# Filling, key order and value spacing in a one-core attention and gated feed-forward kernel

## The chip, the cores and the metric

The kernel runs on one core of one Trainium2 chip. The metric is the device time of one execution in microseconds (us): before the change 269.87, 267.0 and 269.37 us in three runs, median 269.37 us. A further execution was recorded by the hardware profiler.

Five engines of the core run their own instruction lists and wait for each other by semaphores: PE (TensorE, matmuls; its weight loads stand apart as PEld), DVE (VectorE), ACT (ScalarE), POOL (GpSimd) and SP (SyncE, which here only issues DMAs; its rows carry SPq). POOL issues DMAs too.

## The reference

A batch of 4 sequences of 768 tokens has 8 heads of 64 numbers. Each query sees 8 global keys and the 96 keys up to itself; the scores get a penalty by distance and head. The attention's output, as 3072 rows of 512 numbers, goes through a gated feed-forward part.

```python
keep = is_global | is_local                      # pos < 8, or 0 <= rel < 96
scores = scale * q @ k.T - slopes * dist         # -1e9 where not keep
a = softmax(scores)
x = (a @ v).transpose(0, 2, 1, 3).reshape(B * S, H * D)      # 3072 x 512
gate = np.maximum(x @ w_gate, 0.0)               # 512 x 1536
val = x @ w_val
out = (gate * val) @ w_out                       # 1536 x 512
```

## The kernel before, in words

**The pieces.** The work is cut into eight chunks of 384 tokens, the halves of the four sequences (`s` or `c` = 0 to 7; sequence `b = s // 2`). The heads go in four pairs `p`. A sequence's keys are cut into seven tiles of 128 columns: the 8 global keys and 120 others. `kT[b % 2][p]` holds the transposed keys of a pair, `qTb[s % 2]` the transposed queries, with zeros in the other head's half, so that one matmul gives both heads.

**The values.** `vbuf[b % 2]` holds for each of the seven tiles a row of 17 blocks of 64 numbers: ones, values of head 0, ones, values of head 1, and so on to a last block of ones. A matmul with 128 columns of it gives a head's value product in one half of the partitions and the softmax's denominator in the other (`piece_av`, L327). Chunks 0 and 1 use `piece_av_wide` instead (L359), which takes ones from a tile of its own. `fill` (L136) writes ones over a whole tile, and the loads of values (`load_v_globals` L120, `load_v` L131, by POOL) write over the value blocks. `spread_v_globals` (L125, by SP) copies the rows of the global keys from the first tile into the others.

**One chunk of attention.** `piece_qk` makes scores (PE L299), their exponential (ACT L302) and the product with a mask of penalties (DVE L311). It is called three times for a pair, for three groups of key tiles. `piece_av` is called for each head of a pair (`e` = 0, 1): 4 or 5 matmuls, the logarithm of the denominator (ACT L336); with the second head one exponential for both (ACT L341) and two multiplications into `xT` (DVE L344). `av_psum` has two buffers, so the pair's two results are held until L344 has read them.

**Getting queries and keys.** Chunks 0 and 1 are transposed by PE: `piece_cast` (L222, on DVE in chunk 0, on POOL in chunk 1), six small matmuls (`piece_t`, L253), copies out of PSUM on DVE (L258, L259, and `put_keys` L237 to L243; L239 copies the 8 global keys into all seven tiles). From chunk 2 on `early_pieces(s)` does it: POOL casts queries (L266) and keys (L267), SP issues six transposing DMAs (queries L272, keys L275), and POOL puts the keys in order (`piece_order`, L237 to L243). The loads of queries and keys are issued by SP (L110).

**One chunk of feed-forward.** 24 pieces of four matmuls with 384 columns (gate L397, ACT L400; value L407, DVE L409), then six pieces of six matmuls with 512 columns (L416), in pairs; after each pair ACT copies the result (L421) and SP stores it.

**The order.** There is no scheduler: each engine runs its instructions in the order of the program text. `weave` merges lists: `spread` gives the attention pieces of the next chunk evenly spaced places in the current chunk's feed-forward work (0.0 to 0.88 of it, from L503 on), `early_pieces` of the chunk after that stand between 0.25 and 0.75. A list of n pieces is spaced by its length, so two more entries in it move all others. At the beginning (L457 to L470) `aside` says which fills, zeros and loads go ahead of which piece of chunk 0. PE then runs part of chunk 0's feed-forward work with chunk 1's attention in between (L485), a stretch of feed-forward work alone while POOL, SP and the DMAs get chunk 2 ready (L496, L497), and the rest with chunk 2's attention (L500).

Of the kernel before, what the change touches and what calls it, by code (L numbers as in the profile page):

```python
# [15 lines left out]
def kernel(  # L16
# [87 lines left out]
    def load_qk(s, h0, h1):  # L104
# [18 lines left out]
    def spread_v_globals(b, j0=1, j1=NT):  # L123
        t = vbuf[b % 2]
        nc.sync.dma_start(  # L125
            out=t[0:NG, j0:j1, :],
            in_=t[0:NG, 0:1, :].to_broadcast([NG, j1 - j0, (2 * H + 1) * D]))
# [7 lines left out]
    def fill(eng, i, j):  # L135
        eng.memset(vbuf[i][:, j, :].bitcast(mybir.dt.uint32), 0x3F803F80)  # L136
# [33 lines left out]
    fill(nc.vector, 0, 0)  # L170
# [33 lines left out]
    for p in range(2):  # L204
        nc.scalar.copy(qTb[0][64:128, p, 0, :], zeros[64:128])
        nc.scalar.copy(qTb[0][0:64, p, 1, :], zeros[0:64])
# [10 lines left out]
    def piece_cast(s, p):  # L217
        qk = cast_pool.tile([128, 2, NN, 2, D], BF16, name="qk")
        cast_of[s, p] = qk
        for i, src in ((0, qs_of[s]), (1, ks_of[s])):  # L220
# [41 lines left out]
    def piece_cast_all(s, p):  # L262

        qsrc = qs_of[s][:, 2 * p : 2 * p + 2, :].rearrange("t e (n d) -> t e n d", n=NN)
        for e in range(2):
            nc.gpsimd.tensor_copy(qz[s % 2][:, :, p, e, 64 * e : 64 * e + 64], qsrc[:, e])  # L266
        nc.gpsimd.tensor_copy(  # L267
            kc[s % 2].rearrange("t n (h d) -> t h n d", d=D)[:, 2 * p : 2 * p + 2],
            ks_of[s][:, 2 * p : 2 * p + 2, :].rearrange("t e (n d) -> t e n d", n=NN))

    def piece_x(s, n):
# [3 lines left out]
        nc.sync.dma_start_transpose(  # L275
            out=kNb[s % 2][:, :, n * 128 : (n + 1) * 128], in_=kc[s % 2][:, n])
# [95 lines left out]
    def attention_pieces(s):  # L372
# [11 lines left out]
        return QK(0) + QK(1) + AV(0) + QK(2) + AV(1) + QK(3) + AV(2) + AV(3)  # L384
# [68 lines left out]
    def zero_q(i, p):  # L453
        nc.gpsimd.memset(qTb[i][64:128, p, 0, :].bitcast(mybir.dt.uint32), 0)
        nc.gpsimd.memset(qTb[i][0:64, p, 1, :].bitcast(mybir.dt.uint32), 0)

    a0 = attention_pieces(0)  # L457
    aside = {
        1: [lambda: fill(nc.vector, 0, 1), lambda: fill(nc.vector, 0, 2),
            lambda: load_v_globals(0), lambda: load_v(0, 0), lambda: load_v(0, 1)],  # L460
        2: [lambda: nc.vector.memset(kT[0][0][:, 3, 32:128], 0.0), lambda: fill(nc.vector, 0, 3),
# [10 lines left out]
    for j in range(4, NT):  # L472
# [75 lines left out]
```

## Time and profile before

| | us |
|---|---|
| median of three runs (267.0 to 269.87) | 269.37 |
| the profiled execution, its whole time | 267.93 |
| its span, first to last instruction | 266.2 |
| PE busy in the span | 237.6 |
| DVE / ACT / POOL busy | 140.8 / 156.8 / 97.2 |

The profile's views: busy times by engine and by stretch, waits (which instruction stood idle before it, and what released it), and the timeline, whose rows give start, duration, engine, line, what is written and read, how many instructions were merged, and in square brackets the idle time ahead of them. A duration can hold time in which an instruction was held up, so unusual ones are to be looked at beside their neighbours. Line numbers with L are those of the kernel before, unless a text says otherwise; in the changed kernel the same statements stand up to 11 lines further on.

### The profile page before, as it was taken

What the parts mean: (1) busy time and instruction counts of PE and PEld (TensorE: products, weight loads), DVE (VectorE), ACT (ScalarE), POOL (GpSimd) and SP (SyncE); (2) the same over time, 40 slices, a digit from 0 to 9 for tenths busy, and PEclk for the clock granted to TensorE, in tenths of its full rate; (3) what the DMA queues carried; (4) which work ended last, traced back from release to release, by engine and by line L of the source; (5) the groups of instructions that cost most, each with busy time, mean ns of one, the idle gap of its engine ahead of it and who ended that gap; (6) DMA issues with size and microseconds to landing.
All of it is one profiled execution on the core that took longest, in us unless ns stands there. A gap on an engine that the chain in (4) does not pass through costs nothing.

```text
span 266.2 us, 4655 instructions
## 1 busy us (share of the span) xinstructions
PE 237.6 (89%) x1608; PEld 139.1 (52%) x1608; DVE 140.8 (53%) x366; ACT 156.8 (59%) x317; POOL 97.2 (37%) x237
## 2 busy tenths in 40 slices
PE   1268988999699899989999999989998999989994
PEld 0136645666355456645664566545664566546641
DVE  8985895444444366724574376616673366534410
ACT  8338585333367567746775567666774677653321
POOL 8892499050690653244241901516150400000000
PEclk9999999999999999999999999999999999999999
DMA  6999699995896599549629693267928200021012
GB/s 187 163 201 230 149 173 199 248 108 130 239 132 166 169 220 149 115 106 153 209 63 157 72 214 123 59 176 112 233 59 135 106 0 2 0 79 42 0 39 79
DMA packets 81198, 34.56 MB, mean 130 GB/s; under 512 B 56920, under 2 KB 77912, under 8 KB 81176
## 3 DMA queue, kind: packets, MB, share of 16 engines
q1 hardware_dynamic: 49320, 26.38, 36.8%
q0 software_dynamic: 31856, 7.91, 31.2%
q8 instruction: 12, 0.20, 0.3%
q14 instruction: 10, 0.08, 0.1%
HBM read 28.38 MB, written 6.29 MB: 130 GB/s over the span
## 4 chain that ended last, share of the span: by engine, by line
PE 71%; DVE 9%; DMA 6%; ACT 6%; SPq 2%; POOL 2%; issue 2%; DVEq 0%; ACTq 0%; POOLq 0%
PE ff_ps L416 20%; PE ff_ps L407 19%; PE ff_ps L397 19%; PE qk_ps L299 6%; PE av_ps L327 5%; DMA ks<-in_k_dram 5%; ACT lnd L336 2%; DVE xT L344 1%; DVE es L311 1%; DVE kT L239 1%; PE av_ps L359 1%; PE qk_ps L253 1%; SPq L272 1%; ACT rcp L341 1%; SPq L275 1%
## 5 line engine op out<-in xcount | busy, mean ns | idle before, releaser
L397 PE MATMUL ff_ps<-xT,wg 128*128 128x384 bf16 x384 | 78.5, 326 | 1.1 <-DVE xT L344 0.4
L407 PE MATMUL ff_ps<-xT,wv 128*128 128x384 bf16 x384 | 78.0, 326 | 0.0
L409 DVE TENSOR_TENSOR ht<-ff_ps,grelu 128x384 bf16<-128x384 f32 x96 | 53.3, 556 | 34.4 <-PE ff_ps L407 27.3
L400 ACT ACTIVATE grelu<-ff_ps 128x384 bf16<-128x384 f32 x96 | 47.0, 489 | 40.1 <-DVE ht L409 21.8
L416 PE MATMUL ff_ps<-wo_sb,ht 128*128 128x512 bf16 x288 | 68.1, 378 | 0.0
L302 ACT ACTIVATE es<-qk_ps 128x432 bf16<-128x432 f32 (+2 forms) x96 | 49.4, 529 | 28.3 <-PE qk_ps L299 25.9
L311 DVE TENSOR_TENSOR es<-es,m_all 128x432 bf16<-128x432 bf16 (+6 forms) x144 | 43.3, 392 | 29.5 <-ACT es L302 28.7
L344 DVE TENSOR_TENSOR xT<-av_ps,rcp 64x384 bf16<-64x384 f32 x48 | 26.7, 555 | 43.7 <-ACT rcp L341 43.0
L407 PEld LDWEIGHTS <-wv 128*128 128x128 bf16 x384 | 36.4, 98 | 23.4 <-issue 1.1
L397 PEld LDWEIGHTS <-wg 128*128 128x128 bf16 x384 | 36.6, 98 | 22.9 <-issue 0.3
L416 PEld LDWEIGHTS <-ht 128*128 128x128 bf16 x288 | 26.9, 97 | 27.7
L299 PE MATMUL qk_ps<-qT,kT 128*128 128x432 bf16 (+6 forms) x144 | 33.6, 303 | 4.2 <-POOL kT L239 2.6
L336 ACT ACTIVATE lnd<-av_ps 64x384 f32<-64x384 f32 x48 | 23.3, 486 | 9.7 <-PE av_ps L327 8.9
L421 ACT COPY osb<-ff_ps 128x512 f32<-128x512 f32 x24 | 14.1, 586 | 25.1 <-PE ff_ps L416 23.3
L266 POOL CAST qz<-qs 128x192 bf16<-128x192 f32 x48 | 16.3, 367 | 33.6 <-DMA qs<-in_q_dram 26.9
L327 PE MATMUL av_ps<-es,vbuf 128*128 128x216 bf16 (+4 forms) x216 | 20.6, 225 | 5.4 <-DVE xT L344 5.4
L131 POOL DMA_DIRECT2D vbuf<-in_v_dram x28 | 24.4, 879 | 0.8 <-DVE qk L222 0.6
L327 PEld LDWEIGHTS <-vbuf 128*128 128x128 bf16 x216 | 17.6, 97 | 13.6 <-issue 6.9
L299 PEld LDWEIGHTS <-kT 128*128 128x128 bf16 x144 | 14.3, 102 | 16.1 <-issue 3.8
L267 POOL CAST kc<-ks 128x384 bf16<-128x384 f32 x24 | 12.7, 531 | 13.3 <-DMA ks<-in_k_dram 13.3
L253 PE MATMUL qk_ps<-ident,qk 128*128 128x128 bf16 x48 | 5.5, 264 | 12.0 <-DVE qk L222 12.0
L237 POOL COPY kT<-kN 128x360 bf16<-128x360 bf16 x12 | 6.4, 537 | 26.1 <-DMA kN<-kc 26.1
(66 smaller groups left out, 124.9 us busy)
## 6 DMA issues: line engine op xcount, KB each, us to landing
out_dram<-osb SPq DMA_DIRECT2D x24, 256.0 KB, 2.2
qs<-in_q_dram SPq DMA_DIRECT2D x6, 768.0 KB, 6.3
ks<-in_k_dram SPq DMA_DIRECT2D x6, 768.0 KB, 8.6
vbuf<-in_v_dram POOLq DMA_DIRECT2D x24, 120.0 KB, 5.1
qs<-in_q_dram SPq DMA_DIRECT2D x8, 192.0 KB, 9.6
ks<-in_k_dram SPq DMA_DIRECT2D x8, 192.0 KB, 4.2
wg<-in_moe_w_gate_dram POOLq DMA_DIRECT2D x3, 512.0 KB, 5.7
wv<-in_moe_w_val_dram POOLq DMA_DIRECT2D x3, 512.0 KB, 7.5
```

The source lines that it names most:

```text
L131: nc.gpsimd.dma_start(out=v_dst(b, NG + r0, NG + r0 + n, j), in_=v[b, :, KT * j + r0 : KT * j + r0 + n, :].rearrange("h p d -> p h d"))
L299: nc.tensor.matmul(ps[:, c : c + n_], lhsT=kt[:, j, :], rhs=qd[:, :, :, a : a + w], start=True, stop=True)
L302: nc.scalar.activation(es[:, 0:cols], ps[:, 0:cols], AF.Exp, bias=0.0, scale=scale)
L311: nc.vector.tensor_mul(e4, e4, mk)
L327: nc.tensor.matmul(av3[:, :, a : a + w], lhsT=vb[:, j, z0 : z0 + 128], rhs=es[:, c : c + NN * w].rearrange("k (n p) -> k n p", n=NN), star ...
L336: nc.scalar.activation(ln[o0 : o0 + 64], av[d0 : d0 + 64, 0:QH], AF.Ln, bias=0.0, scale=1.0)
L344: nc.vector.tensor_tensor(xT_of[s][r, p, :], av_of[s, p, e_][r, 0:QH], rc[r], op=ALU.mult)
L397: nc.tensor.matmul(psg[:, 0:QH], lhsT=w_of(wg, dc, fc), rhs=xT[:, dc, :], start=(dc == 0), stop=(dc == N_DC - 1))
L400: nc.scalar.activation(gr, psg[:, 0:QH], AF.Relu, bias=0.0, scale=1.0)
L407: nc.tensor.matmul(psv[:, 0:QH], lhsT=w_of(wv, dc, fc), rhs=xT[:, dc, :], start=(dc == 0), stop=(dc == N_DC - 1))
L409: nc.vector.tensor_tensor(ht[:, fc, :], psv[:, 0:QH], st["gr"], op=ALU.mult)
L416: nc.tensor.matmul(ps2, lhsT=ht[:, fc, n * 128 : (n + 1) * 128], rhs=wo_sb[:, fc, :], start=(fc == 0), stop=(fc == N_FC - 1))
```

## The change

1. `fill` is gone. The value tiles of sequence 0 get no ones (chunks 0 and 1 don't read them); POOL clears the last tile, which no load fills wholly. Four fills on DVE and three on POOL at the beginning go away. The tiles of sequence 1 get their ones by `fill_ones`, which writes the nine blocks of ones alone (on POOL, after one clearing of the last tile); those of `vbuf[0]` get them later, on DVE, for sequence 2.
2. `spread_v_globals` copies only the value blocks, by one DMA for each tile: three and three in sequence 0, six in each of the others, in place of one DMA.
3. Keys are loaded ahead of queries in each pair of loads, and cast ahead of them. `early_pieces` does all keys' casts, then the three key transposes, then the queries' casts and transposes, then the ordering of keys: 18 pieces in place of 11.
4. The zeros in `qTb[0]` for pairs 2 and 3 are written by ACT, not POOL.
5. In chunks 2 to 7 the last pieces come in another order: the two value pieces of pair 2 stand between the three score pieces of pair 3, and two empty pieces ahead of the value pieces of pair 3.

```diff
-        for src, dst in ((q, qs_of[s]), (k, ks_of[s])):
+        for src, dst in ((k, ks_of[s]), (q, qs_of[s])):
...
     def spread_v_globals(b, j0=1, j1=NT):
-        t = vbuf[b % 2]
-        nc.sync.dma_start(
-            out=t[0:NG, j0:j1, :],
-            in_=t[0:NG, 0:1, :].to_broadcast([NG, j1 - j0, (2 * H + 1) * D]))
+        for j in range(j0, j1):
+            nc.sync.dma_start(out=v_dst(b, 0, NG, j), in_=v_dst(b, 0, NG, 0))
...
-    def fill(eng, i, j):
-        eng.memset(vbuf[i][:, j, :].bitcast(mybir.dt.uint32), 0x3F803F80)
+    def fill_ones(eng, i, j):
+        eng.memset(vbuf[i][:, j, :].bitcast(mybir.dt.uint32).rearrange(
+            "p (h z) -> p h z", z=D // 2)[:, 0 : 2 * H + 1 : 2, :], 0x3F803F80)
...
-    fill(nc.vector, 0, 0)
...
     def early_pieces(s):
-        out = [(0.0, lambda p=p: piece_cast_all(s, p)) for p in range(HP)]
-        out += [(0.0, lambda n=n: piece_x(s, n)) for n in range(NN)]
+        out = [(0.0, lambda p=p: piece_cast_k(s, p)) for p in range(HP)]
+        out += [(0.0, lambda n=n: piece_xk(s, n)) for n in range(NN)]
+        out += [(0.0, lambda p=p: piece_cast_q(s, p)) for p in range(HP)]
+        out += [(0.0, lambda n=n: piece_xq(s, n)) for n in range(NN)]
         out += [(0.0, lambda p=p: piece_order(s, p)) for p in range(HP)]
...
-        return QK(0) + QK(1) + AV(0) + QK(2) + AV(1) + QK(3) + AV(2) + AV(3)
+        g = QK(3)
+        a = AV(2)
+        return (QK(0) + QK(1) + AV(0) + QK(2) + AV(1) + g[0:1] + a[0:1] + g[1:2] + a[1:2] + g[2:3]
+                + [(0.0, lambda: None)] * 2 + AV(3))
...
-    for j in range(4, NT):
-        fill(nc.gpsimd, 0, j)
+    nc.gpsimd.memset(vbuf[0][:, NT - 1, :].bitcast(mybir.dt.uint32), 0)
...
+    nc.gpsimd.memset(vbuf[1][:, NT - 1, :].bitcast(mybir.dt.uint32), 0)
     for j in range(NT):
-        fill(nc.gpsimd, 1, j)
+        fill_ones(nc.gpsimd, 1, j)
...
-    weave(f1_0[G[1]] + f1_1[G[1]], spread(early_pieces(2), 0.0, 1.0))
+    weave(f1_0[G[1]] + f1_1[G[1]], spread(early_pieces(2), 0.0, 1.0),
+          [(0.1 + 0.12 * j, lambda j=j: fill_ones(nc.vector, 0, j)) for j in range(NT)])
```

**How the order moves, first place: ACT at the end of a chunk's attention** (here chunk 3's, woven into chunk 2's feed-forward work; `es` are the exponentials of scores, `lnd` and `rcp` the logarithm and the reciprocal of `piece_av`, each `osb` the end of two feed-forward pieces L416). Before:

```order
L302 ACTIVATE es_1614<-qk_ps 128x480
L400 ACTIVATE grelu<-ff_ps 128x384
L302 ACTIVATE es_1631<-qk_ps 128x480
L302 ACTIVATE es_1654<-qk_ps 128x432
L421 COPY osb<-ff_ps 128x512
L336 ACTIVATE lnd<-av_ps 64x384 x2
L341 ACTIVATE rcp<-lnd 128x384
L336 ACTIVATE lnd<-av_ps 64x384
L421 COPY osb<-ff_ps 128x512
L336 ACTIVATE lnd<-av_ps 64x384
L341 ACTIVATE rcp<-lnd 128x384
L421 COPY osb<-ff_ps 128x512
```

and of the change:

```order
L309 ACTIVATE es_1609<-qk_ps 128x480
L411 ACTIVATE grelu<-ff_ps 128x384
L343 ACTIVATE lnd<-av_ps 64x384
L411 ACTIVATE grelu<-ff_ps 128x384
L309 ACTIVATE es_1648<-qk_ps 128x480
L343 ACTIVATE lnd<-av_ps 64x384
L348 ACTIVATE rcp<-lnd 128x384
L309 ACTIVATE es_1686<-qk_ps 128x432
L432 COPY osb<-ff_ps 128x512
L343 ACTIVATE lnd<-av_ps 64x384
L432 COPY osb<-ff_ps 128x512
L343 ACTIVATE lnd<-av_ps 64x384
```

The logarithms and the reciprocal of pair 2 now stand ahead of the first `osb`, and pair 3's first logarithm behind it: on PE, three pieces L416 and one score piece lie between the last value matmul of pair 2 and the first of pair 3, where before there was one piece L416.

**Second place: POOL at the beginning,** from its first load of values on. Before:

```order
L120 DMA vbuf_98<-in_v_dram 8x8x64
L131 DMA vbuf_98<-in_v_dram 120x8x64 x4
L454 MEMSET qT_109 64x192
L455 MEMSET qT_109 64x192
L147 DMA wg_117<-in_moe_w_gate_dram 128x4x512
L147 DMA wv_120<-in_moe_w_val_dram 128x4x512
L136 MEMSET vbuf_98 128x544 x3
```

(the pair of zeros stands twice there) and of the change, down to the second group of loads:

```order
L120 DMA vbuf_98<-in_v_dram 8x8x64
L129 DMA vbuf_98<-in_v_dram 120x8x64 x4
L146 DMA wg_117<-in_moe_w_gate_dram 128x4x512
L146 DMA wv_120<-in_moe_w_val_dram 128x4x512
L478 MEMSET vbuf_98 128x544
L481 MEMSET kT_0_101 128x36
...
L129 DMA vbuf_98<-in_v_dram 120x8x64 x2
```

The zeros are gone from between the loads of values and those of weights, one memset of a value tile is left of three, and the loads of values have no fill on DVE to wait for.

**Third place: SP, from the loads of chunk 2's queries and keys to those of chunk 3.** Before:

```order
L110 DMA qs<-in_q_dram 128x8x192
L110 DMA ks<-in_k_dram 128x8x192
L125 DMA vbuf_99<-vbuf_99 8x6x1088
L272 DMA_TRANSPOSE qT_109<-qz_113 128x8x128
L275 DMA_TRANSPOSE kN_111<-kc_115 128x4x128
...
L110 DMA qs<-in_q_dram 128x8x192
```

and of the change:

```order
L110 DMA ks<-in_k_dram 128x8x192
L110 DMA qs<-in_q_dram 128x8x192
L125 DMA vbuf_99<-vbuf_99 8x8x64 x6
L275 DMA_TRANSPOSE kN_111<-kc_115 128x4x128 x3
L279 DMA_TRANSPOSE qT_109<-qz_113 128x8x128 x3
L110 DMA ks<-in_k_dram 128x8x192
```

Query and key transposes alternated; now the three of the keys come first, behind six small copies in place of one.

More of the change, by code (lines that the diff above doesn't have):

```diff
@@ L203, with zero_q @@
     nc.vector.tensor_scalar(dd[0:NG, 0], gd, BIG, float(NL), op0=ALU.mult, op1=ALU.max)
-    for p in range(2):
-        nc.scalar.copy(qTb[0][64:128, p, 0, :], zeros[64:128])
-        nc.scalar.copy(qTb[0][0:64, p, 1, :], zeros[0:64])
+    def zero_q(i, p):
+        nc.scalar.copy(qTb[i][64:128, p, 0, :], zeros[64:128])
+        nc.scalar.copy(qTb[i][0:64, p, 1, :], zeros[0:64])
+    zero_q(0, 0)
+    zero_q(0, 1)
     for h in range(H):
@@ L478 @@
     for p in range(HP):
-        zero_q(1, p)
+        nc.gpsimd.memset(qTb[1][64:128, p, 0, :].bitcast(mybir.dt.uint32), 0)
+        nc.gpsimd.memset(qTb[1][0:64, p, 1, :].bitcast(mybir.dt.uint32), 0)
     load_w_group(1)
```

26 lines of the change are left out of this document (12 added, 14 removed).

## Prediction

> **What bounds the kernel now.** First the busy time by stretch, to see where PE, the busiest engine, is not at work: the beginning, the stretch up to chunk 2's scores, and the feed-forward work of chunks 2 to 6 with the attention of 3 to 7.
>
> ```profile
> core 0: us, PE busy (x) PEld busy (x) DVE busy (x) ACT busy (x) POOL busy (x), PEclk, DMA share, GB/s
> 0.00:26.30 26.30, 12.44 (x106) 7.94 (x107) 20.43 (x68) 16.54 (x33) 19.60 (x44) 1.00 1.25 195
> 26.30:67.10 40.80, 38.35 (x304) 23.10 (x301) 24.80 (x69) 20.37 (x42) 20.09 (x42) 1.00 1.02 170
> ...
> 93.40:239.00 145.60, 140.81 (x935) 83.35 (x935) 78.13 (x192) 95.89 (x194) 42.46 (x110) 1.00 0.58 116
> ```
>
> The clock is 1.00 throughout. From 26.3 us on PE has work nearly all the time, and what it doesn't spend on matmuls lies in few waits; in the first 26.3 us it is busy for less than half, behind DVE, which is busy for 20.43 us. So the change can win in two places: PE's waits, and DVE's list at the beginning. The waits of PE:
>
> ```profile
> PE qk_ps L253 <- DVE qk L222: 12.0, 4, 4.3
> PE av_ps L327 <- DVE xT L344: 5.4, 7, 1.0
> PE qk_ps L299 <- POOL kT L239: 2.6, 1, 2.6
> ```
>
> The columns are total, times, longest. The first is the beginning; the other two are what parts 3 and 5 of the change aim at.
>
> **Value spacing: -4.8 us.** In feed-forward work alone, one product on DVE for two groups of four matmuls:
>
> ```profile
> 65.22 0.56 DVE L409 TENSOR_TENSOR ht<-ff_ps,grelu 128x384 bf16<-128x384 f32 x1 [0.74 <-PE ff_ps L407]
> ```
>
> That is 1.30 us for two groups, 0.65 for one. And one of the seven waits for L344, in chunk 3's attention:
>
> ```profile
> 114.80 0.77 PE L327 MATMUL av_ps<-es,vbuf 128*128 128x72 bf16 x10
> ...
> 115.61 1.00 ACT L336 ACTIVATE lnd<-av_ps 64x384 f32<-64x384 f32 x2
> ...
> 116.64 0.52 ACT L341 ACTIVATE rcp<-lnd 128x384 f32<-128x384 f32 x1
> ...
> 117.20 1.14 DVE L344 TENSOR_TENSOR xT<-av_ps,rcp 64x384 bf16<-64x384 f32 x2 [2.54 <-ACT rcp L341]
> ...
> 117.80 0.46 PE L327 MATMUL av_ps<-es,vbuf 128*128 128x72 bf16 x5 [0.93 <-DVE xT L344]
> ...
> 146.78 0.42 PE L327 MATMUL av_ps<-es,vbuf 128*128 128x216 bf16 x4 [0.99 <-DVE xT L344]
> ```
>
> Both value pieces of pair 2 run back to back, end at 115.57, and the first buffer is free at 117.8, 2.2 us later; PE has one piece of six matmuls in between (117.80 - 0.93 - 115.57 = 1.30) and then stands for 0.93. Each of the five chunks 3 to 7 has this wait, at 0.93 or 0.99: 3 x 0.93 + 2 x 0.99 = 4.77 us. In the changed order PE has three such pieces and a score piece, over 3.9 us, between the end of pair 2 and the start of pair 3, so 2.2 us fit with 1.7 to spare. What is late next: the first value piece of pair 2 is now earlier, behind pair 1 by three groups of four matmuls (3 x 0.65) and two score matmuls, some 2.2 us; it needs the release of one buffer alone, whose chain is one L336, L341 and the first half of L344, 0.50 + 0.52 + 0.57 = 1.6. That holds by 0.6 us, unless a relu or a store's copy gets ahead on ACT (some 0.5 each). In chunk 2's attention (the other two of the seven waits, 0.6 us together) the pieces have 1.5 us between pairs 1 and 2, so I leave a wait of that size there. The removed waits count in full: PE is the bound in those 145.6 us (140.81 busy), with DVE and ACT at half to two thirds.
>
> **Keys first: -2.65 us.** The one wait for keys is at chunk 2's first score:
>
> ```profile
> 52.10 0.64 POOL L266 CAST qz<-qs 128x192 bf16<-128x192 f32 x2 [5.94 <-DMA qs<-in_q_dram]
> ...
> 56.41 0.51 POOL L267 CAST kc<-ks 128x384 bf16<-128x384 f32 x1 [3.67 <-DMA ks<-in_k_dram]
> ...
> 59.60 1.35 SPq L272 DMA_TRANSPOSE qT<-qz  x1
> ...
> 66.31 1.26 SPq L275 DMA_TRANSPOSE kN<-kc  x1
> ...
> 68.80 0.54 POOL L237 COPY kT<-kN 128x360 bf16<-128x360 bf16 x1 [8.77 <-DMA kN<-kc]
> ...
> 69.71 0.36 PE L299 MATMUL qk_ps<-qT,kT 128*128 128x432 bf16 x1 [2.65 <-POOL kT L239]
> ```
>
> and, from the DMA issues, the median time to land of the two kinds of transpose:
>
> ```profile
> qT<-qz SPq DMA_TRANSPOSE x18, 2.8
> kN<-kc SPq DMA_TRANSPOSE x18, 2.3
> ```
>
> The queries land at 52.1, the keys at 56.4, then six transposes of about 1.3 us each on SP (59.6 to 67.6), 2.3 to land, and one pair's ordering (0.9): 69.7, where PE wanted 67.06. After the change the first of the two loads, now the keys, should land near 52.1. Four casts (4 x 0.51) end at 54.2; SP issues three transposes from there, and if the second has to wait for the queries' load they end at 58.9; keys in SBUF at 61.2. The queries' eight casts take 56.4 to 59.0, their transposes 59.0 to 62.9, landed by 65.7. POOL orders keys at 61.2 to 64.5. So both are there 1.4 us ahead of 67.06, and the whole 2.65 go. The casts on POOL are as many as before; all twelve no longer stand ahead of the first transpose.
>
> In the later chunks this chain is hidden now and stays so: for chunk 4 it runs
>
> ```profile
> 104.05 0.51 POOL L267 CAST kc<-ks 128x384 bf16<-128x384 f32 x1 [4.12 <-DMA ks<-in_k_dram]
> ...
> 116.80 0.54 POOL L237 COPY kT<-kN 128x360 bf16<-128x360 bf16 x1 [8.67 <-DMA kN<-kc]
> ...
> 122.94 0.35 PE L299 MATMUL qk_ps<-qT,kT 128*128 128x432 bf16 x1
> ```
>
> with the first pair's keys ready at 117.6, five ahead of the need; by the same steps as above the last transposes now land near 113.
>
> **The beginning: -2.0 us, the least sure term.** Three timelines of one engine each, DVE, POOL and PE:
>
> ```profile
> 4.59 1.09 DVE L136 MEMSET vbuf<- 128x544 uint32 x2
> ...
> 6.84 0.55 DVE L239 COPY kT<-kT 128x56 bf16<-128x56 bf16 x1
> ...
> 10.08 3.29 DVE L239 COPY kT<-kT 128x56 bf16<-128x56 bf16 x1
> ...
> 15.80 0.18 DVE L239 COPY kT<-kT 128x56 bf16<-128x56 bf16 x1
> ...
> 19.56 0.37 DVE L239 COPY kT<-kT 128x56 bf16<-128x56 bf16 x1
> ```
>
> ```profile
> 4.65 2.74 POOL L131 DMA_DIRECT2D vbuf<-in_v_dram  x3
> ...
> 10.00 0.78 POOL L147 DMA_DIRECT2D wg<-in_moe_w_gate_dram  x1
> 10.77 0.77 POOL L147 DMA_DIRECT2D wv<-in_moe_w_val_dram  x1
> 11.52 1.56 POOL L136 MEMSET vbuf<- 128x544 uint32 x3
> 13.00 0.34 POOL L476 MEMSET kT<- 128x36 uint32 x4
> ```
>
> ```profile
> 4.32 0.82 PE L253 MATMUL qk_ps<-ident,qk 128*128 128x128 bf16 x6 [4.32 <-DVE qk L222]
> 7.92 0.82 PE L253 MATMUL qk_ps<-ident,qk 128*128 128x128 bf16 x6 [2.78 <-DVE qk L222]
> ...
> 13.63 0.82 PE L253 MATMUL qk_ps<-ident,qk 128*128 128x128 bf16 x6 [3.48 <-DVE qk L222]
> ```
>
> Four fills of 0.55 (1.09 for two) leave DVE. The two at 4.59 end at 5.68, while the transposes that the next copy waits for were through at 5.14: 0.5 us. The first stands ahead of the setup, while the first loads are under way, the last within the hold-up of L239 at 6.84; without that cover they would be 0.55 each.
>
> The larger thing is L239. Alone it takes 0.18; at 10.08 it takes 3.29, and ends at 13.38 when POOL's unbroken run of two weight loads, three fills and four memsets ends (13.34). At 6.84 it takes 0.55 and ends with the third of POOL's value loads (both 7.39); at 19.56, 0.37. The casts behind it release PE. In the change POOL's run is longer: four value loads (2.74 for three) without a wait from 4.65 to 8.3, weight loads to 9.85, one memset (1.56 for three) and the four small ones to 10.7. The first L239 comes at 6.45, within the second value load. Two ends: it is let in at the end of that load or the next (6.5 to 7.4), as at 6.84; the second one then meets the memsets at 9.4 and is let in at 10.7, where it was 13.38; the third transposes start 2.3 earlier, of which casts beside POOL's eight zero memsets take back 0.3: -2.0. Or it is held to 10.7, as at 10.08; then the second transposes start at 10.9 in place of 7.92, the second L239 ends as before, but scores and masks are not yet done behind it, and the third transposes start at 15.2 in place of 13.63: +1.5. The first L239 is nearest to the row at 6.84, the same copy in the same kind of load; I take -2.0.
>
> The Trainium skill, SBUF — State Buffer, Who interferes with whom, says that such a copy and a POOL instruction take a shared port by an exclusive lock for one instruction each, and whoever starts first blocks the other. By that rule alone the sum is the -2.0 here; the 3.29 us over nine POOL instructions is more than the rule allows, and with that row the sum would be +1.5.
>
> **What costs nothing.** The one row that this part needs besides is SP's copy of global values:
>
> ```profile
> 8.05 0.90 SPq L125 DMA_DIRECT2D vbuf<-vbuf  x1
> ```
>
> Four zero copies on ACT (0.50 each, as an L336 of half the partitions) stand around the first scores' exponentials, while DVE is behind; beside a free DVE they would be 2 us. The 19 small copies more on SP, at the 0.9 of this row at most, stand in SP's waits for POOL ahead of the transposes (59.60, with the queries' first cast at 52.10). Seven `fill_ones` on DVE, half a fill each, lie where DVE idles 0.74 of every 1.30 us; without that cover they would be 2 us. POOL's fills get shorter by about 1 us, ahead of nothing that PE waits for.
>
> **Sum.** -4.77 - 2.65 - 2.0 = -9.4; with an earlier beginning, loads that already keep the DMAs at a share of 1.02 may not follow, which I put at +0.6: -8.8. The profiled execution took 267.93 (span 266.2, 1.7 around it): 259.1. The median of the runs stands 1.4 above that execution, inside their spread of 2.9; I add half: 259.8 us.
>
> **The rivals.** A row for the last of them, the loads of global values, with the median time to land:
>
> ```profile
> vbuf<-in_v_dram POOLq DMA_DIRECT2D x4, 8.0 KB, 3.4
> ```
>
> *L239 held.* The beginning gives +1.5 in place of -2.0. For it: the row at 10.08. Against it: those at 6.84 and 19.56. 259.8 + 3.5 = 263.3. *Keys or queries still late.* If the first of two loads doesn't land earlier when it is the keys', or the queries' transposes, now last, end after 67.06, the 2.65 stay: 262.4. For it: only 1.4 us of slack in my chain, and a beginning that is 2 us earlier eats them; against it: six transposes were behind both loads, now three are. *The value wait moves.* If pair 2's first piece waits for pair 1 as pair 3 did, the 4.8 come back: 264.6. Against it: 0.6 us of slack in each chunk; for it: ACT's list is denser there. *Slower: the small copies hold up SP.* Each of the six spread copies could wait for the one before. The place is SP ahead of the key transposes in chunks 2, 4 and 6, its price six landings. A load of 8 KB of values takes 3.4 us to land; six are 20, less the 2 now, so keys come 18 late, against a slack of 10 in chunks 4 and 6 (113 to 122.9) and 1.4 in chunk 2: stalls of 8, 8 and 17, some 293 us. It decides from about 2.1 us each, where the stalls reach 9.4 and no gain is left. Against it: the L125 row has 0.90, and nothing behind it reads the copies but value pieces a chunk later.
>
> **How the numbers follow.** The forecast 0.52, L239 held 0.25, keys or queries late 0.10, value wait moved 0.08, slower 0.03, some of the smaller mishaps together 0.02. Two of the rivals at once reach 267. The range 256.8 to 264.8: below, the forecast without the 0.6, with the 0.6 us of chunk 2's waits and with no half of the median's distance, and a little for the spread; above, L239 held with the runs' spread over it. A change of 1% (2.7 us) is about what these runs can tell from none. Faster by more: 0.93, within 1% 0.04, slower 0.03.
>
> **What would show it.** Right: no idle of PE ahead of L327 of pair 3 in chunks 3 to 7; chunk 2's first score directly behind a feed-forward piece; the third set of transposes at 11 to 12 us; PE's busy time as before, 237 to 238. Wrong: an L239 (L240 there) of 3 us or more that starts at 6.4; a wait of L327 in front of pair 2; SP rows of the small copies over 2 us; score matmuls that wait for query transposes.

## The result, and the profile after it

The changed kernel takes 258.73 us (median of 4 runs, 258.07 to 259.28); the kernel before takes 269.62 (median of 4, 267.0 to 271.33). The ratio is 0.963, with a 95% interval of 0.955 to 0.970. The profiled execution took 258.44 us, with a span of 256.7; before it was 267.93 and 266.2. The forecast was 259.8, in a range of 256.8 to 264.8.

First the busy time by stretch of the changed kernel, cut at the same work as the three stretches of before. The columns are stretch, its length, then the busy time and the number of instructions of each engine, PE's clock, and the DMAs:

```profile
0.00:24.70 24.70, 11.88 (x106) 7.66 (x107) 17.47 (x63) 18.48 (x37) 15.78 (x36) 1.00 1.32 196
24.70:65.80 41.10, 38.21 (x304) 23.16 (x303) 26.85 (x76) 20.34 (x43) 25.81 (x60) 1.00 1.10 191
89.20:229.55 140.35, 139.75 (x932) 82.87 (x931) 78.73 (x192) 96.10 (x194) 39.60 (x107) 1.00 0.53 117
```

DVE has 17.47 us of work in the beginning where it had 20.43. The second stretch ends at chunk 2's first score; before, the wait of 2.65 us came behind it. The last stretch is 5.25 us shorter with the same matmuls, and PE is idle for 0.6 us of it, where it was idle for 4.8. Then the waits of PE in the changed kernel (total, times, longest):

```profile
PE qk_ps L254 <- DVE qk L223: 9.1, 3, 4.5
PE qk_ps L254 <- DVE ks L158: 1.7, 1, 1.7
...
PE qk_ps L254 <- POOL qk L223: 0.8, 1, 0.8
...
PE av_ps L334 <- DVE xT L351: 0.5, 1, 0.5
```

The wait for ordered keys at chunk 2 is gone from the list. Of seven waits of the value matmuls (5.4 us) one of 0.5 is left. In the beginning PE waits for 10.8 us in place of 12.0, and a wait of 0.8 for a cast on POOL is new.

The same place as the 0.99 us wait shown of before, chunk 4's attention within chunk 3's feed-forward work:

```profile
137.36 0.31 PE L306 MATMUL qk_ps<-qT,kT 128*128 128x288 bf16 x2
137.51 2.75 PE L427 MATMUL ff_ps<-wo_sb,ht 128*128 128x512 bf16 x12
140.10 0.42 PE L334 MATMUL av_ps<-es,vbuf 128*128 128x216 bf16 x4
140.38 1.46 PE L427 MATMUL ff_ps<-wo_sb,ht 128*128 128x512 bf16 x6
141.67 0.42 PE L334 MATMUL av_ps<-es,vbuf 128*128 128x216 bf16 x4
```

No row has an idle time behind it in brackets: twelve output matmuls, 2.6 us, stand where six stood. And the way of the keys and queries to chunk 2, on SP and POOL, with the first score on PE:

```profile
46.54 4.63 SPq L125 DMA_DIRECT2D vbuf<-vbuf  x6
52.68 5.13 SPq L275 DMA_TRANSPOSE kN<-kc  x3
58.00 3.93 SPq L279 DMA_TRANSPOSE qT<-qz  x3
```

```profile
50.80 1.85 POOL L264 CAST kc<-ks 128x384 bf16<-128x384 f32 x4 [7.91 <-DVE vbuf L134]
54.53 2.38 POOL L272 CAST qz<-qs 128x192 bf16<-128x192 f32 x8 [1.88 <-DMA qs<-in_q_dram]
59.03 0.54 POOL L238 COPY kT<-kN 128x360 bf16<-128x360 bf16 x1 [2.12 <-DMA kN<-kc]
```

```profile
65.16 0.81 PE L408 MATMUL ff_ps<-xT,wg 128*128 128x384 bf16 x4
65.81 0.35 PE L306 MATMUL qk_ps<-qT,kT 128*128 128x432 bf16 x1
```

The first pair's keys are in order at 59.9, six microseconds ahead of the score at 65.81, which stands directly behind its product. The six small copies take 0.77 each. The view puts the wait of the first cast of keys down to a memset on DVE; most other traces of this order put it down to the load of the keys, which the cast reads.

Where the time came from, by the starts of the same work in the two traces:

| stretch | before | after | difference | term of the sum |
|---|---|---|---|---|
| start to first feed-forward matmul | 26.00 | 24.45 | -1.55 | -2.0 |
| to the third group of gates | 32.45 | 32.91 | +0.46 | +0.6 |
| to chunk 2's feed-forward work | 33.90 | 30.79 | -3.11 | -2.65 |
| chunk 2's feed-forward work | 29.94 | 28.45 | -1.49 | -0.93 or -0.99 |
| chunks 3 to 6 | 116.52 | 112.76 | -3.76 | four of these |
| chunk 7 to the end | 27.35 | 27.32 | -0.03 | 0 |
| span | 266.16 | 256.68 | -9.48 | -8.8 |

### The profile page after: what moved, and what is told of

It is laid out like the page before. It is cut to its first block, busy times and chain, and to the rows that moved or that the text cites. A ratio compares the mean times of both kernels' runs of the same rounds, so it can differ in the third digit from the quotient of the medians.

```text
span 256.7 us, 4693 instructions
## 1 busy us (share of the span) xinstructions
PE 236.1 (92%) x1608; PEld 138.7 (54%) x1608; DVE 140.9 (55%) x369; ACT 159.0 (62%) x321; POOL 93.6 (36%) x232
## 3 DMA queue, kind: packets, MB, share of 16 engines
q1 hardware_dynamic: 50816, 26.16, 38.0%
## 4 chain that ended last, share of the span: by engine, by line
PE 77%; DVE 11%; DMA 5%; ACT 3%; issue 1%; SPq 1%; POOL 0%; DVEq 0%; ACTq 0%; POOLq 0%
PE ff_ps L427 24%; PE ff_ps L418 22%; PE ff_ps L408 21%; PE av_ps L334 5%; PE qk_ps L306 4%; DMA ks<-in_k_dram 4%; DVE xT L351 2%; DVE es L318 2%; DVE ht L420 2%; PE qk_ps L254 1%; DVE qk L223 1%; DMA qs<-in_q_dram 1%; ACT lnd L343 1%; ACT rcp L348 1%; DVE qT L260 1%
## 5 line engine op out<-in xcount | busy, mean ns | idle before, releaser
L427 PE MATMUL ff_ps<-wo_sb,ht 128*128 128x512 bf16 x288 | 67.1, 379 | 0.0
L351 DVE TENSOR_TENSOR xT<-av_ps,rcp 64x384 bf16<-64x384 f32 x48 | 26.7, 555 | 45.7 <-ACT rcp L348 41.2
L343 ACT ACTIVATE lnd<-av_ps 64x384 f32<-64x384 f32 x48 | 23.3, 485 | 11.1 <-PE av_ps L334 10.4
L432 ACT COPY osb<-ff_ps 128x512 f32<-128x512 f32 x24 | 14.0, 585 | 24.4 <-PE ff_ps L427 23.5
L129 POOL DMA_DIRECT2D vbuf<-in_v_dram x28 | 24.4, 879 | 0.8 <-issue 0.4
L272 POOL CAST qz<-qs 128x192 bf16<-128x192 f32 x48 | 14.8, 356 | 3.6 <-DMA qs<-in_q_dram 3.6
L348 ACT ACTIVATE rcp<-lnd 128x384 f32<-128x384 f32 x24 | 12.5, 522 | 0.8
```

What stands on the lines that cost most here:

```text
L129: nc.gpsimd.dma_start(out=v_dst(b, NG + r0, NG + r0 + n, j), in_=v[b, :, KT * j + r0 : KT * j + r0 + n, :].rearrange("h p d -> p h d"))
L343: nc.scalar.activation(ln[o0 : o0 + 64], av[d0 : d0 + 64, 0:QH], AF.Ln, bias=0.0, scale=1.0)
L351: nc.vector.tensor_tensor(xT_of[s][r, p, :], av_of[s, p, e_][r, 0:QH], rc[r], op=ALU.mult)
L427: nc.tensor.matmul(ps2, lhsT=ht[:, fc, n * 128 : (n + 1) * 128], rhs=wo_sb[:, fc, :], start=(fc == 0), stop=(fc == N_FC - 1))
```

## The experiments

### Each part alone

**Spacing alone**, on the kernel before:

```diff
-        return QK(0) + QK(1) + AV(0) + QK(2) + AV(1) + QK(3) + AV(2) + AV(3)
+        g = QK(3)
+        a = AV(2)
+        return (QK(0) + QK(1) + AV(0) + QK(2) + AV(1) + g[0:1] + a[0:1] + g[1:2] + a[1:2] + g[2:3]
+                + [(0.0, lambda: None)] * 2 + AV(3))
```

> The kernel before with the new order of attention pieces alone (pair 3's scores among pair 2's value pieces, two empty pieces ahead of pair 3's value pieces). Theory, buffer release: pair 3's first value piece waited for the two buffers of pair 2, whose chain takes 2.2 us, and now has over 3.9 us of matmuls in between; the five waits of 0.93 or 0.99 go, the span falls by 4.8 to 5.2 us to 261.0 to 261.4, and everything up to chunk 3's first score stays at its times. Rival, the wait moves: pair 2's first value piece, now nearer to pair 1, waits in place of pair 3's; the total of waits for L344 stays near 5.4 us and the span near 266.

Measured: 265.92 us (263.63 to 266.29, 4 runs) against 268.99 for the kernel before; ratio 0.986 (0.982 to 0.991). The waits ahead of pair 3 went as the theory has it: chunks 3 to 6 take 112.76 us, exactly as in the changed kernel. But only 1.7 us of the expected 4.8 reached the end of the profiled execution (span 264.4). Most of the rest went in two places. The first is chunk 2's first score, PE's rows and then the granted clock (the column ahead of the DMA share) by stretch:

```profile
70.46 0.48 PE L299 MATMUL qk_ps<-qT,kT 128*128 128x432 bf16 x1 [3.06 <-POOL kT L239]
70.72 1.49 PE L410 MATMUL ff_ps<-xT,wv 128*128 128x384 bf16 x4
```

```profile
66.00:70.40 4.40, 1.39 (x9) 0.61 (x7) 0.66 (x2) 0.98 (x2) 0.85 (x4) 1.00 0.56 114
70.40:74.00 3.60, 3.54 (x13) 1.75 (x14) 1.32 (x3) 1.17 (x3) 3.20 (x10) 0.53 1.04 345
74.00:78.00 4.00, 4.00 (x27) 2.13 (x26) 2.28 (x7) 2.21 (x6) 4.00 (x9) 1.00 1.35 141
```

Behind a wait of 3.06 us, where the trace of before has 2.65, the clock falls to about half for some 3.4 us, and a product of four matmuls takes twice as long as its 0.65. The one run of this kernel at a clock of 1.000 took 263.63 us (span 261.8, where 261.0 to 261.4 was expected), the three at 0.994 took 265.74 to 266.29.

The second is at the end of chunk 2's attention, on SP, ACT and PE:

```profile
82.29 1.29 SPq L272 DMA_TRANSPOSE qT<-qz  x1
...
88.94 1.26 SPq L275 DMA_TRANSPOSE kN<-kc  x1
90.31 1.00 SPq L425 DMA_DIRECT2D out_dram<-osb  x2
```

```profile
92.66 0.59 ACT L424 COPY osb<-ff_ps 128x512 f32<-128x512 f32 x1 [2.91 <-DMA out_dram<-osb]
93.27 0.99 ACT L336 ACTIVATE lnd<-av_ps 64x384 f32<-64x384 f32 x2
```

```profile
96.04 0.32 PE L400 MATMUL ff_ps<-xT,wg 128*128 128x384 bf16 x1 [0.91 <-DVE xT L344]
```

Six transposes stand one behind the other in SP's queue, the output stores behind them, so ACT's next copy waits 2.91 us for its buffer with the last values' logarithm behind it, and PE waits 0.91 for that. The kernel before has the same row with 0.42. With keys first the queue is broken:

```profile
72.64 5.24 SPq L275 DMA_TRANSPOSE kN<-kc  x3
77.98 1.32 SPq L433 DMA_DIRECT2D out_dram<-osb  x2
79.41 4.00 SPq L279 DMA_TRANSPOSE qT<-qz  x3
```

That is the changed kernel: two stores go between the two sets, and the wait is gone. In chunk 2's feed-forward work spacing alone gains 0.08 us, the keys' order alone 0.60, both together 1.49: there the spacing needs the keys' order.

**Keys first alone**, on the kernel before (with the casts and transposes split into those of keys and those of queries, as in the change, and keys cast ahead of queries in chunks 0 and 1 too):

```diff
-        for src, dst in ((q, qs_of[s]), (k, ks_of[s])):
+        for src, dst in ((k, ks_of[s]), (q, qs_of[s])):
...
-        out = [(0.0, lambda p=p: piece_cast_all(s, p)) for p in range(HP)]
-        out += [(0.0, lambda n=n: piece_x(s, n)) for n in range(NN)]
+        out = [(0.0, lambda p=p: piece_cast_k(s, p)) for p in range(HP)]
+        out += [(0.0, lambda n=n: piece_xk(s, n)) for n in range(NN)]
+        out += [(0.0, lambda p=p: piece_cast_q(s, p)) for p in range(HP)]
+        out += [(0.0, lambda n=n: piece_xq(s, n)) for n in range(NN)]
```

> The kernel before with keys loaded, cast and transposed ahead of queries alone. Theory: only the 2.65 us wait ahead of chunk 2's first score goes; span 263.1 to 263.7, later chunks unchanged to 0.2 us. Rival, the keys came earlier in the changed kernel because SP and POOL had less to do and the beginning was earlier: the order alone then leaves a wait of 1 us or more at the same place, span 264.6 or more. Second rival, queries become the late ones: a wait for the query transposes of about the same 2.65 us, span 266.

Measured: 264.76 us (264.72 to 264.93, 4 runs) against 268.99; ratio 0.984 (0.981 to 0.987); span 263.0. Theory right: no wait for keys or queries is left at chunk 2, the stretch to its feed-forward work is 2.83 us shorter, chunk 2's own 0.60 (0.42 of it the wait behind the stores), and later chunks are unchanged. The wait behind the stores was not foreseen. Neither rival is left. The beginning became 0.6 us longer (first feed-forward matmul at 26.60, before 26.00), with a cast of queries that waits 0.37 us for its load; by the third group of gates 0.3 of that remains.

**The beginning alone** (the changed kernel with the two other parts undone):

> The changed kernel with the order of keys and queries and the order of attention pieces as before: what is left is the beginning without fills of ones, the small copies of the global values and the moved zeros. Theory: the first feed-forward matmul comes 1.0 to 1.6 us earlier (24.4 to 25.0 in place of 26.0), and 0.5 to 1.1 of that is left at 42 us. Whether it reaches the end: if chunk 2's keys follow the earlier beginning, span 265.1 to 265.7; rival, the keys' loads are issued and land at their old times, so that the 2.65 us wait grows by what the beginning won: span 266.0 to 266.4. Second rival, the small copies cost on SP: span over 266.5.

Measured: 267.40 us (266.33 to 267.96, 6 runs) against 268.99; ratio 0.992 (0.989 to 0.995). The profiled execution had a span of 266.2, to the microsecond that of before, although its first feed-forward matmul came at 23.32 us, 2.7 earlier, and its third group of gates 1.9 earlier. Its rows at chunk 2:

```profile
68.24 0.54 PE L300 MATMUL qk_ps<-qT,kT 128*128 128x432 bf16 x1 [3.08 <-POOL kT L240]
68.57 1.49 PE L407 MATMUL ff_ps<-xT,wv 128*128 128x384 bf16 x4
69.85 0.57 PE L300 MATMUL qk_ps<-qT,kT 128*128 128x432 bf16 x1
70.21 1.29 PE L397 MATMUL ff_ps<-xT,wg 128*128 128x384 bf16 x4
```

The wait for keys grew by 0.43, and the matmuls behind it, which took 2.48 us from first score to first output product (69.71 to 72.19 before), took 3.90: 1.42 more. Together 1.85, all of the lead. So the span that the rival gives came out in this execution, but by luck: the rival has the wait grow by the whole lead, and it grew by 0.43, while the clock, in neither theory, took 1.42. The keys followed the earlier beginning for the greater part, as the theory has it, and the lead itself was larger than the 1.0 to 1.6 us expected. In the two runs with a clock of 0.998 and 0.997 the kernel took 266.33 and 266.37 us, some 1.2 less than the 267.59 that is the median of the kernel before at full clock (next section). Which of parts 1, 2 and 4 of the change brings this was not tried.

### Does the idle time lower the clock?

Over the three comparisons the kernel before ran 39 times: 12 times at a granted clock of 0.999 or more (266.47 to 268.25 us), 27 times at 0.987 to 0.994 (267.74 to 270.21). This kernel fills its wait:

```diff
+    def busy_pe():
+        ps = qk_psum.tile([128, 512], FP32, name="qk_ps")
+        for i in range(12):
+            nc.tensor.matmul(ps[:, 0:QH], lhsT=w_of(wg, i % N_DC, 0), rhs=xT_of[1][:, i % N_DC, :],
+                             start=True, stop=True)
...
+        if (s, p, g) == (2, 0, 0):
+            busy_pe()
```

> The kernel before with twelve spare matmuls of 0.16 us (a first gate weight by chunk 1's attention output, result unused) ahead of chunk 2's first score, so that PE works through about 2 of the 2.65 us that it waits there. Theory, the idle time lowers the clock: the wait that is left is about 0.7 us, the granted clock is 0.997 or more in every run, and the times lie at 267.2 to 268.5, where the kernel before reaches 269 to 270 in its runs at a clock of 0.994. Rival, the clock falls there whether PE idles or not: about half of the runs or more at a clock of 0.994 or less, times spread over 267.7 to 270 as before.

Measured: 267.80 us (267.06 to 269.11) in 12 runs, all 12 at 0.997 or more; the kernel before 269.34 (17 runs, 6 of them at 0.999 or more); ratio 0.997 (0.994 to 1.000). PE's rows:

```profile
66.30 2.11 PE L291 MATMUL qk_ps<-xT,wg 128*128 128x384 bf16 x12
69.19 0.36 PE L307 MATMUL qk_ps<-qT,kT 128*128 128x432 bf16 x1 [0.77 <-POOL kT L239]
```

The keys come no earlier against the work ahead of them. Theory right as to the clock: all 12 runs are at 0.997 or more, where 27 of the 39 of the kernel before are not. The time is less clear. The medians differ by 1.5 us, but the interval of the ratio reaches 1.000, and at full clock the kernel before is as fast (median of its 12 such runs 267.59). What the spare matmuls do is to take the slower of two outcomes away.

When the clock falls is best seen in the trace of the beginning alone, by stretch, with the clock again ahead of the DMA share:

```profile
65.20:67.76 2.56, 0.00 (x0) 0.00 (x0) 0.00 (x0) 0.49 (x1) 0.43 (x1) 1.00 0.60 115
67.76:68.24 0.48, 0.00 (x1) 0.01 (x1) 0.00 (x0) 0.00 (x0) 0.48 (x4) 0.50 0.38 85
```

It falls at 67.76, after 2.6 us without a matmul and ahead of the score at 68.24, and stays at 0.50 for 3.41 us, to 71.17; with spacing alone it falls at 70.56 and stays there as long, to 73.97. In both traces the full clock ahead of the fall is on record for 47.79 us, which is 14 times 3.413. If the clock is set in steps of 3.413 us (an estimate from these traces), the step that ends at 67.76 held 0.8 us of matmuls and 2.6 of idle time. In the trace of before, whose record of the clock begins at 23.82, the 13th step ends at 68.19 and cuts the wait of 2.65 us into 1.1 and 1.5; there the clock stayed. So a wait of this length may lower the clock or not, by where it lies against the steps. One such fall is a mean clock of 0.994 over 266 us, which is that of most of the 27 slower runs; none of those was traced.

In the changed kernel, without that wait, no run of the ten in this study is below 0.997. It need not be the only cause, though: of the kernels below, whose traces have no such wait either, six runs lie at 0.991 to 0.993 (one without empty pieces, four without mixing, one with earlier loads), and no trace shows where.

### What the empty pieces do

**Without them**, on the changed kernel:

```diff
-                + [(0.0, lambda: None)] * 2 + AV(3))
+                + AV(3))
```

> The changed kernel without the two empty pieces; the scores of pair 3 stay among the value pieces of pair 2. Theory, buffer release: between the end of pair 2 and the start of pair 3 stand one score group and one product of six matmuls, 0.36 + 1.30 = 1.7 us, against a chain of 2.2: a wait of about 0.5 in each of five chunks, 2.5 us in all, so 261.2 where the changed kernel has 258.7 (span 259.2). Rival, the mixing of scores and values is what removes the wait: no wait, span 256.7.

Measured: 265.74 us (265.14 to 267.18, 4 runs), span 263.4: 6.7 more than the changed kernel's span, where I expected 2.5. Its waits:

```profile
PE av_ps L334 <- DVE es L318: 3.4, 6, 0.6
PE av_ps L334 <- DVE xT L351: 3.4, 6, 0.6
```

The 0.6 for the buffers are there; a second wait, for the masked scores, is as large, and I had not seen it. ACT and DVE at one of the six places:

```profile
140.74 0.48 ACT L343 ACTIVATE lnd<-av_ps 64x384 f32<-64x384 f32 x1
141.26 0.52 ACT L348 ACTIVATE rcp<-lnd 128x384 f32<-128x384 f32 x1
141.69 0.43 ACT L309 ACTIVATE es<-qk_ps 128x336 bf16<-128x336 f32 x1
```

```profile
141.81 1.14 DVE L351 TENSOR_TENSOR xT<-av_ps,rcp 64x384 bf16<-64x384 f32 x2 [2.03 <-ACT rcp L348]
142.99 0.40 DVE L318 TENSOR_TENSOR es<-es,m_all 128x288 bf16<-128x288 bf16 x2
```

Pair 2's last value piece and pair 3's last score group run next to each other on PE, so their chains queue on ACT and on DVE, and the masks come last. Mixing without distance is worse than the order of before.

**One empty piece:** `[(0.0, lambda: None)]` in place of the two.

> The changed kernel with one empty piece in place of two. Now two products of 1.30 us and a score group lie between the end of pair 2 and pair 3's value pieces, over the 2.2 us of the buffers' chain, but one product only, 1.30 us, between pair 3's last score group and the value matmuls that read it. Theory, two bounds of which the later one counts: in the kernel without empty pieces these matmuls went on 2.8 us after that score group, so the wait for the buffers goes and the wait for the masks (es L318) grows to 1.1 to 1.2 us in each of five or six chunks: 264 to 266, no better than without empty pieces. Rival, the two waits add and one of them is gone: 0.6 us a chunk, 261 to 262. Second rival, the buffers are all: no wait, 258.7.

Measured: 258.82 us (258.70 to 259.00, 4 runs), no wait at the place in chunks 3 to 7. My theory fell, and the rival that adds the waits with it; the second rival had the number. The delay of 2.8 us between score group and masks was no constant: with one empty piece a product of 1.30 us comes between value piece and score group too, their chains no longer meet, and the masks end at 141.1, as the matmuls that read them start. One empty piece is just enough; two leave a margin.

**Two empty pieces and no mixing:**

```diff
+        return (QK(0) + QK(1) + AV(0) + QK(2) + AV(1) + QK(3) + AV(2)
+                + [(0.0, lambda: None)] * 2 + AV(3))
```

> The changed kernel with the two empty pieces and without the mixing: pair 3's three score groups, then pair 2's two value pieces, the two empty pieces, pair 3's value pieces. Theory: the distance alone does it. Ahead of pair 3's value pieces lie two products of 1.30 us, 2.6 us against a chain of 2.2, and pair 3's masks are done long before: no wait, 258.7 us as the changed kernel, within 1 us. Rival, the mixing is needed: the waits for L351 come back at 0.5 to 0.95 us in each of five chunks, 261.2 to 263.5.

> The kernel with the two empty pieces and without the mixing once more, since three of its four runs lay at 260.0 to 260.6 with a clock of 0.993 and the profiled one at 258.2 with a clock of 1.000. Theory, the mixing of scores and values is worth nothing and the runs differ in a fall of the clock after an idle stretch of PE in the first microseconds or at chunk 2's first score, where the order of these pieces plays no part: most of the runs now at the full clock, or a profile whose clock falls before 75 us. Rival, it is the order without mixing that loses clock: again more than half of the runs near 260.3, with the fall in the attention of chunks 2 to 7.

Measured: spans of 256.5 and 256.1 in the two profiles, with no wait for L351 in either list; medians 260.24 us (258.23 to 260.57, 4 runs) and 258.50 (257.91 to 260.34, 6 runs). Without disturbance the mixing is worth nothing, and the distance is all. But four of these ten runs had a clock of 0.993 and took 260.0 to 260.6 us. None of the changed kernel's ten had such a clock, though one of them took 260.47 us at 0.997. Neither profile shows the fall, so where it comes from stays open.

### What holds the key copy

Three memsets of before's length put back into POOL's list of the changed kernel:

```diff
+    for j in range(4, NT):
+        nc.gpsimd.memset(vbuf[1][:, j, :].bitcast(mybir.dt.uint32), 0)
     nc.gpsimd.memset(vbuf[0][:, NT - 1, :].bitcast(mybir.dt.uint32), 0)
```

> The changed kernel with three whole-tile memsets (tiles of the second value buffer, written again later) put back in POOL's list between the second weight load and the zeros of the last tile, as long as the three fills of the kernel before. Theory, the hold lasts for POOL's run: the second key copy L240, which starts near 10.1 us, is held until POOL's memsets end near 11.6 to 12.0, and the third set of transposes starts at 13.5 to 14.2 in place of 12.1; 1 to 1.5 us at the first feed-forward matmul, of which little more than 1 is left at the end: 259.5 to 260. Rival, one instruction at most: the copy is let in behind the memset that it meets, 0.6 us at most, and the third transposes start by 12.7; 258.7 to 259.3.

Measured: 258.33 us (258.13 to 259.25, 4 runs). POOL, then DVE:

```profile
9.47 1.58 POOL L479 MEMSET vbuf<- 128x544 uint32 x3
10.94 0.60 POOL L480 MEMSET vbuf<- 128x544 uint32 x1
11.43 0.54 POOL L483 MEMSET kT<- 128x36 uint32 x4
```

```profile
10.38 1.21 DVE L240 COPY kT<-kT 128x56 bf16<-128x56 bf16 x1
```

The copy starts in the second of four large memsets and ends at 11.59, as the fourth does (11.54): past two ends of an instruction, so one instruction is not the limit, but ahead of the end of the four small memsets, where before it was held through those too. In time it cost nothing that shows, and the third transposes came at 12.24, so the rival has the times and the theory the longer hold: I had overrated what stands behind the copy. The hold is about POOL instructions that follow each other without a gap; what ends it, neither theory says.

### The loads of chunk 1

```diff
-        13: [lambda: load_qk_after(1, True)],
+        11: [lambda: load_qk_after(1, True)],
```

> The changed kernel with the loads of chunk 1's queries and keys issued two pieces earlier (at piece 11 in place of 13). Theory, these loads are what takes back half a microsecond of the gain at the beginning: they are issued about 1.5 us earlier, chunk 1's first casts follow, the 0.82 us wait at its second set of transposes goes, and the time is 258.0 to 258.4. Rival, the DMAs are full there: the loads land no earlier or delay the first weights and values, 258.7 to 260.

> The changed kernel itself, beside the others on one chip. Expected: 258.1 to 259.3 as in its four runs, and a clock of 0.997 or more in nearly all runs, since no wait of PE after 26 us is longer than 1 us.

> The changed kernel with chunk 1's loads two pieces earlier, once more and with more rounds: its profile was 1.2 us shorter (the 0.82 us wait at chunk 1's second transposes gone), its four runs only 0.2. If the shorter profile is its own: 257.2 to 257.8 median, 1 us below the changed kernel on the same chip. If not: equal within 0.4.

Measured: 258.48 us (257.19 to 258.95, 4 runs), then 258.00 (257.46 to 258.45, 4 runs) beside 258.67 (257.95 to 260.47, 6 runs) for the changed kernel on the same chip. In the first trace of it the second transposes of chunk 1 follow at once, where the changed kernel waits 0.82 us:

```profile
26.00 0.81 PE L408 MATMUL ff_ps<-xT,wg 128*128 128x384 bf16 x4
26.65 0.50 PE L254 MATMUL qk_ps<-ident,qk 128*128 128x128 bf16 x6
```

In the second trace a wait of 0.5 for a POOL cast is there again. From the first feed-forward matmul to the third group of gates these two traces take 32.30 and 32.65 us, the two of the changed kernel 32.91 and 32.29, the kernel before 32.45. So it is not shown that these loads take back half a microsecond: in its second trace the changed kernel loses nothing there. The gain, 0.7 us in that comparison, lies between the two outcomes that were expected and within the spread of the runs, and it is not settled that this version is faster.

The changed kernel's own six runs went over what was expected of them twice, 259.51 and 260.47 us, both at a clock of 0.997 as expected. So these two have another cause than such a fall of the clock, and it stays open.

## Why the prediction was right, and where its sizes were off

**Value spacing, -4.8: right in place and size.** Chunks 3 to 6 gained 0.98, 0.91, 0.97 and 0.90, against 0.93 or 0.99. Next in line should have been a wait of pair 2 for pair 1, with 0.6 us of slack: it held in chunks 3 to 7. In chunk 2's attention, where a wait of about 0.6 was to stay, that wait of pair 2 came, with 0.46; before, the 0.6 stood ahead of pair 3. Not seen: pair 3's own masks as a second bound on the distance, which the two empty pieces cover and none would have failed; and some 0.5 us that chunk 2 gained besides, from stores that no longer stand behind six transposes.

**Keys first, -2.65: right.** 2.83 alone, 3.11 in the whole. Casts, transposes and ordering ran in the forecast order and 1 to 2.2 us earlier than in my chain, since the keys' casts began at 50.80 rather than 52.1. The first pair's keys had 5.9 us of slack, where the chain gives 5.0; the chain's 1.4 is that of the queries, whose landing the trace doesn't show, but the last of their transposes is issued by 61.9, one microsecond ahead of the chain, and the score waits for nothing. Both small rivals (keys late, queries late) had no hold.

**The beginning, -2.0: right in kind, too large by half a microsecond here.** Neither L240 is held for long, as I chose. In the changed kernel the first takes 0.18 us, its time alone, and ends at 6.82, at a load's end (6.81); in five other traces it takes 0.63 to 0.90. The second takes 0.18 too and ends at 10.30 and not at 10.7. But casts behind them were slowed:

```profile
7.10 0.80 DVE L223 CAST qk<-qs 128x384 bf16<-128x384 f32 x1
...
11.37 0.70 DVE L223 CAST qk<-qs 128x384 bf16<-128x384 f32 x1
```

0.29 to 0.34 is what such a cast took before where nothing held it. The first ends 0.2 us behind a POOL load's end. So the third transposes start at 12.14, 1.5 earlier and not 2.3; in the changed kernel's second trace the second of these casts takes 0.35 and they start at 11.79. In the nine other traces with this beginning, some with one edit in it, the first feed-forward matmul comes at 23.3 to 24.4, 1.6 to 2.7 earlier than before, so -2.0 is a fair mean. The earliest of them is the one without keys first, which alone cost 0.6 there in its one trace; my term leaves that out. The +0.6 for loads that don't follow was 0.46 in this trace and -0.16 in the second one of the changed kernel, so that term is not confirmed. Taken together the two fit: the third group of gates starts at 57.85 to 58.78 us in the four traces with the old beginning and at 56.55 to 57.99 in the seven with the new one unedited, 1.3 earlier in the mean, where the sum has 1.4.

I also read the clock as 1.00 throughout. The view prints 1.00 where the trace has no record of it, and the records begin only at 23.82 us in the kernel before and at 21.33 in the changed one. The same matmuls, a little ahead of that and a little behind it, in the changed kernel:

```profile
20.56 0.71 PE L366 MATMUL av_ps<-es,ones 128*64 128x216 bf16 x8
...
21.86 0.45 PE L366 MATMUL av_ps<-es,ones 128*64 128x216 bf16 x8 [0.21 <-ACT lnd L372]
```

So PE is slower for the first 20 us or so, before and after alike; what that costs the beginning no run shows.

**From the execution to the median, +0.7: wrong.** I took the 1.4 us between the median and the profiled execution of before as spread of the runs and kept half of it. It was mostly the clock: in the 39 later runs of the kernel before the median is 269.46 us at 0.987 to 0.994 and 267.59 at 0.999 or more, and the profiled execution is of the second kind. The clocks of the three runs behind the forecast are not on record, but two of their times lie with the first kind and one with the second. Filling the 2.65 us wait removed the first kind, and the change, which removes the wait, did too. The changed kernel's median lies 0.3 above its profiled execution. The Trainium skill, TensorE: Matmul & The Clock Gate, HAM oscillation — how this bites in real kernels, says that idle gaps of PE above about 3.4 us bring the clock back to half. Here waits of 3.06 and 3.08 us were enough, the clock fell 2.6 us into the second of them, and the stretch at 0.50 lasted 3.41 us; by the rule alone the 2.65 us of before would be safe. The Trainium skill, TensorE: Matmul & The Clock Gate, What's actually happening, has the window run free of the kernel, which would explain why the same wait is hit in some runs only. The 47.79 us on record in two traces, 14 times 3.413, agree with a fixed window; no run here shows where it lies in an execution that was not traced.

**The slower rival** needed 2.1 us for each small copy. They took 0.77 each ahead of chunk 2 and 1.1 ahead of chunk 4 (one of the 24 took 2.26), with keys far ahead of their need.

The sum was -8.8 against -9.5 measured on the profiled execution: -0.5 in value spacing and chunk 2's stores, -0.5 at the keys, +0.3 in the beginning with what it gave back. Three signs that I had named came out otherwise. The third transposes start at 12.14, just outside 11 to 12 us. A wait ahead of pair 2, a sign of being wrong, is there in chunk 2, with 0.46. PE's busy time, 237.6 us before, is 236.1 and not 237 to 238, with 1608 matmuls in both traces: 0.6 of that lies in the beginning, where the record of the full clock starts earlier (21.33 us in place of 23.82), and much of the rest can be that a group of four is given 0.81 us ahead of a wait and 0.65 ahead of other matmuls (an estimate: seven waits fewer make 1.1). Nothing rests on it.

## What to carry to other kernels

Ask of each wait of PE how long it is, not only what it adds up to: a wait of 2.6 to 3 us can cost half as much again in slow matmuls behind it, shows in some runs only, and an earlier start elsewhere can push it over the edge and lose all it won. When the consumer of a double buffer comes too early, put other work between, and check the distance from each thing that it reads, the masks as well as the buffers. A queue that carries several kinds of transfers passes its delays on: splitting six transposes into two sets let the stores through and freed an engine that seemed to have nothing to do with them.

## What the runs showed of the hardware that was not expected

- PE's clock falls to 0.50 for 3.41 us at an idle stretch of 3.06 or 3.08 us, once after 2.6 us of it, and matmuls that keep PE busy for 2 of 2.65 us prevent it in 12 of 12 runs.
- A DVE copy that takes 0.18 us alone took 3.29 us beside nine POOL instructions without a gap, 1.21 beside three large memsets, and 0.4 to 0.9 beside single loads or memsets.
- Six transposes of 128x128 take PE 0.82 us at 4.47 and 0.50 at 26.16. The trace has no record of the clock ahead of 21.33 us, and the view prints 1.00 there; the matmuls just before and behind that time (0.71 and 0.45) say that the clock is lower at first.
